# Batches 0 and 1 of a sparse-attention and feed-forward kernel in finer attention phases, and batch 1 hosted by all of tile 0

## The chip, the cores and the metric

The kernel runs on one core of a Trainium2 chip. The metric is the device time of one execution in microseconds (us), as the median of several runs. Engines are named as in the profile: PE is the matmul engine (PEld its weight loads), DVE the vector engine, ACT the scalar engine, POOL the GpSimd engine, SP the engine whose queue issues the loads. The stores are issued from ACT's queue.

## The reference, cut to what matters

Eight batches of 8 heads, 576 positions, head size 64. Heads 0 to 3 look at the last 32 positions (local), heads 4 to 7 at the earlier positions with the same remainder modulo 32 (strided). The result goes through a multiplicative feed-forward stage.

```python
mask_local = (rel >= 0) & (rel < 32)                       # rel = i - j
mask_strided = (rel >= 0) & (j % 32 == i % 32)
scores = where(mask, q @ k.T / 8, -1e9)
x = softmax(scores) @ v                                    # (8, 8, 576, 64) -> (4608, 512)
a = x @ w1; b = x @ w2                                     # 512 -> 1024
out = ((a * b) @ w3) @ w_out                               # 1024 -> 1024 -> 512
```

## The kernel before, in words

**Attention.** A batch is worked in four pairs of heads (hp 0 and 1 local, 2 and 3 strided). The positions of a pair are cut into blocks: 6 of 96 queries (local) or 8 of 72 queries (strided, positions regrouped by remainder), so that only near-diagonal blocks of the scores are computed. A pair has five phases. T (ph_T, L215) transposes q and k of the pair on PE into the PSUM tile pt, and for the first pair of a batch also the last 64 positions of all heads (the rest, R, L232); copies bring them to qT and kT. S (ph_S, L258) computes the scores of all blocks into sps, with the last blocks of each head in pt. The soft part (ph_soft, L278) is an exponential on ACT in two instructions (L286) and one multiplication with the mask on DVE (L287) into ptm. PV (ph_PV, L291) multiplies ptm with v, which carries a column of ones, and DVE divides by the sum: reciprocal (L312), multiplication into xqs (L313); call these two the norm. T2 (ph_T2, L316) transposes xqs, and a copy (L74 or L327 on ACT, L76 on DVE) puts it into xT, the input of the feed-forward stage. Phase function ph_TS (L418) joins S of a pair with T of the next one.

**Feed-forward.** w3 and w_out do not depend on the data, so the kernel first multiplies them into w34 (the fold: fold_tr L389 transposes a block of w3, fold_mm L398 multiplies). Then the 4608 tokens go in 9 tiles of 512. A tile has 24 units: 8 times a (L348) and b (L357), four matmuls of 512 columns each, with the product on DVE (L359), and 8 halves of the output (L371, ops), four matmuls each. Tile t needs the attention of batches 0 to t.

**Order of the work.** PE's program is written out by hand. The attention phases stand in a list, stream, with GAP marks. host (L450) emits the units of the fold or of a tile and takes the phases up to the next marks after each unit. The fold hosts batch 0. Ten of tile 0's a and b units run alone, the other 14 units host batch 1; tile t hosts batch t+1 for t from 1 to 6. T of the next batch's first pair and its S stand at the end of the batch before, except for batches 0 and 1, which both begin with a T of their own.

**Loads.** SP's queue issues the loads in program order; each goes to one of 9 staging tiles in float32 and is cast to float16 by POOL (L78 t for w3, q and k; L185, L196 for v; w2h) or by ACT (w1h, L74). DMA completion semaphores go round in 8 lanes that loads and stores share, so an issue waits for the transfer 8 back. The order at the start is: w3 and w_out with batch 0 between them, w1 and w2 in four parts with batch 1's first q and k group (heads 0 to 3) and rest before the last part, then v of batch 1's local heads (v16L), the second q and k group (heads 4 to 7), v of its strided heads (v16S), and batch 2.

**PSUM.** Eight banks: psF 3 (units), psA 2 (sps, used again by PV), psT 2 (pt), psM 1 (T2, and the last strided block of PV, pm).

## Time and profile before

| | |
|---|---|
| runs | 292.54, 294.87, 295.78 us; median 294.87 us |
| the profiled execution | 296.77 us, its span 295.1 us, mean granted PE clock 0.975 |
| busy, share of the span | PE 90%, DVE 50%, ACT 51%, POOL 35% |
| the fold with batch 0 | to about 48 us |
| tile 0 with batch 1 | about 48 to 84 us |
| tiles 1 to 6 with batches 2 to 7 | about 84 to 250 us |
| tiles 7 and 8 alone | to the end |

The profile's page is one execution. Its view by slices shows busy shares over time, the windows view gives busy time and granted clock for chosen stretches, the timeline lists instructions with the idle time in front of them and what released them (in brackets), the waits view sums such idle time. In a timeline row the first number is the start, the second the time from the start of the first to the end of the last of the instructions that are taken together. The ends of matmuls are modelled, so the distance from one start to the next is the better duration for PE.

### The profile page before, as it was taken

To read this page: it belongs to the slowest core of one execution; us is meant where nothing else is said; L and a number is where in the kernel's file an instruction comes from. 1 tells how busy PE (TensorE), PEld (TensorE's weight loads), DVE (VectorE), ACT (ScalarE), POOL (GpSimd) and SP (SyncE) were. 2 spreads that over 40 slices of the span, in tenths; PEclk is the share of its full clock that TensorE was granted. 3 is DMA by queue.
4 is the path that set the end of the run, shared out by engine and by line. 5 is a ranking of instruction groups with operands and counts; after the bars stand their busy time and mean duration, and the time that the engine had idled before them with its cause. 6 is when DMAs were issued, how large, how long until landed. Compare 5 with 4: busy or idle time off the path is not lost.

```text
span 295.1 us, 6686 instructions
## 1 busy us (share of the span) xinstructions
PE 264.6 (90%) x2689; PEld 135.8 (46%) x2689; DVE 148.4 (50%) x279; ACT 150.2 (51%) x309; POOL 104.6 (35%) x118
## 2 busy tenths in 40 slices
PE   2468987997779999999999999999999999999995
PEld 1133543444445554555455455545554554444442
DVE  2016563474556774765558567646654663330420
ACT  2025784467545556556565655555555655323332
POOL 5649644565445833557566424110000000000000
PEclk9988997999959999999999999999999999999999
DMA  7999999996879957997989892120011002103003
GB/s 247 346 219 344 302 347 264 216 265 122 270 233 224 253 106 206 264 180 243 259 172 286 177 273 49 36 109 3 0 73 74 0 2 107 38 0 138 4 3 142
DMA packets 58656, 48.68 MB, mean 165 GB/s; under 512 B 29184, under 2 KB 49664, under 8 KB 58624
## 3 DMA queue, kind: packets, MB, share of 16 engines
q1 hardware_dynamic: 53440, 38.81, 53.9%
q10 hardware_dynamic: 5184, 9.44, 8.9%
q8 instruction: 21, 0.34, 0.5%
q14 instruction: 11, 0.09, 0.1%
HBM read 38.80 MB, written 9.44 MB: 163 GB/s over the span
## 4 chain that ended last, share of the span: by engine, by line
PE 71%; ACT 10%; DMA 8%; DVE 5%; issue 3%; POOL 1%; SPq 1%
PE bps L357 21%; PE aps L348 20%; PE ops L371 17%; ACT pte L286 4%; PE sps L308 4%; DMA st<-in_moe_w_dram 3%; DMA st<-in_moe_w_out_dram 3%; PE sps L266 2%; DVE ptm L287 2%; PE ps L320 2%; ACT osb L382 2%; PE pt L224 2%; DVE xqs L313 1%; DMA out_dram<-osb 1%; PE pt L266 1%
## 5 line engine op out<-in xcount | busy, mean ns | idle before, releaser
L348 PE MATMUL aps<-xT,w1h 128*128 128x512 f16 x288 | 77.0, 386 | 3.6 <-ACT xT L327 3.6
L351 ACT COPY asb<-aps 128x512 f32<-128x512 f32 x72 | 43.0, 597 | 67.0 <-PE aps L348 65.3
L357 PE MATMUL bps<-xT,w2h 128*128 128x512 f16 x288 | 75.7, 386 | 0.0
L359 DVE TENSOR_TENSOR abt<-bps,asb 128x512 f16<-128x512 f32 x72 | 49.6, 689 | 50.1 <-PE bps L357 48.0
L371 PE MATMUL ops<-w,abt 128*128 128x512 f16 x288 | 68.5, 379 | 0.0
L78 POOL CAST t<-st 128x1024 f16<-128x1024 f32 (+1 forms) x48 | 48.2, 1011 | 32.7 <-DMA st<-in_k_dram 14.5
L357 PEld LDWEIGHTS <-w2h 128*128 128x128 f16 x288 | 26.9, 99 | 35.0 <-issue 7.7
L286 ACT ACTIVATE pte<-sps 128x960 f16<-128x960 f32 (+1 forms) x32 | 31.7, 990 | 19.1 <-PE sps L266 18.0
L348 PEld LDWEIGHTS <-w1h 128*128 128x128 f16 x288 | 26.7, 100 | 28.7 <-issue 1.9
L371 PEld LDWEIGHTS <-abt 128*128 128x128 f16 x288 | 25.9, 98 | 27.7
L185 POOL CAST v16L<-st 32x768 f16<-32x768 f32 (+1 forms) x32 | 27.9, 872 | 22.0 <-PE aps L348 7.6
L382 ACT COPY osb<-ops 128x512 f32<-128x512 f32 x36 | 21.5, 598 | 25.8 <-PE ops L371 25.8
L313 DVE TENSOR_TENSOR xqs<-sps,rcp 96x768 f16<-96x768 f32 (+1 forms) x32 | 32.6, 1018 | 0.7
L287 DVE TENSOR_TENSOR ptm<-pte,maskL 128x1152 f16<-128x1152 f16 x16 | 13.6, 852 | 28.7 <-ACT pte L286 28.7
L287 DVE TENSOR_TENSOR ptm<-pte,maskS 72x1152 f16<-72x1152 f16 x16 | 14.8, 928 | 25.6 <-ACT pte L286 25.6
L74 ACT COPY qT<-pt 128x256 f16<-128x256 f16 (+2 forms) x64 | 23.3, 410 | 7.7 <-PE pt L232 4.5
L196 POOL CAST v16S<-st 72x1024 f16<-72x1024 f32 x16 | 17.8, 1116 | 21.5 <-PE pm L308 11.6
L308 PEld LDWEIGHTS <-ptm 72*128 72x128 f16 (+1 forms) x448 | 18.2, 98 | 14.7 <-DVE ptm L287 7.1
L371 PE MATMUL ops<-woh,w3T 128*128 128x512 f16 x64 | 19.6, 438 | 2.1 <-POOL woh L78 1.2
L266 PEld LDWEIGHTS <-kT 64*128 64x128 f16 x448 | 10.1, 97 | 16.2 <-issue 10.6
L320 PEld LDWEIGHTS <-xqs 72*128 72x128 f16 (+1 forms) x224 | 12.0, 99 | 8.1 <-DVE xqs L313 1.6
L76 DVE COPY kT<-pt 128x128 f16<-128x128 f16 (+1 forms) x28 | 11.5, 435 | 7.5 <-ACT qT L74 7.5
(53 smaller groups left out, 201.1 us busy)
## 6 DMA issues: line engine op xcount, KB each, us to landing
out_dram<-osb ACTq DMA_DIRECT2D x36, 256.0 KB, 2.0
st<-in_moe_w_dram SPq DMA_DIRECT2D x16, 512.0 KB, 8.7
st<-in_q_dram SPq DMA_DIRECT2D x16, 512.0 KB, 5.3
st<-in_k_dram SPq DMA_DIRECT2D x16, 512.0 KB, 6.3
st<-in_v_dram SPq DMA_DIRECT2D x32, 144.0 KB, 7.1
st<-in_v_dram SPq DMA_DIRECT2D x16, 256.0 KB, 7.4
st<-in_moe_w_out_dram SPq DMA_DIRECT2D x4, 512.0 KB, 8.1
st<-in_q_dram SPq DMA_DIRECT2D x8, 128.0 KB, 7.8
```

Of the source, the lines that this page charges most:

```text
L78: nc.gpsimd.tensor_copy(out=out, in_=in_)
L185: nc.gpsimd.tensor_copy(out=vt[pr, hs, :, 0:D], in_=st[pr])
L286: nc.scalar.activation(out=pte[0:kr, lo:hi], in_=src, func=AF.Exp, bias=0.0, scale=scale)
L287: nc.vector.tensor_mul(ptm[0:kr, 0:2 * S].rearrange("p (a x) -> p a x", x=w), pte[0:kr].rearrange("p (a x) -> p a x", x=w), _ap(mk, 0, [[m ...
L308: pe(nc.tensor.matmul(xps[:, h, i * 65:i * 65 + 65], s.ptm[0:kr, c0:c0 + P], vt[0:kr, 2 * (s.hp % 2) + h, c, :], start=True, stop=True))
L313: nc.vector.tensor_mul(s.xqs[0:w, cs[0]:cs[0] + l].rearrange("p i h d -> p h i d"), xv[:, :, :, 0:D], _ap(rcp, 0, [[rcp.ap[0][0], w], [ST, ...
L348: pe(nc.tensor.matmul(aps, w1h[:, ci, bass.ds(jc * P, P)], xT[ci][:, tok], start=(ci == 0), stop=(ci == KM - 1)))
L351: nc.scalar.copy(out=asb, in_=aps)
L357: pe(nc.tensor.matmul(bps, w2h[:, ci, bass.ds(jc * P, P)], xT[ci][:, tok], start=(ci == 0), stop=(ci == KM - 1)))
L359: nc.vector.tensor_mul(abts[tch][:, jc, :], bps, st["asb"])
L371: pe(nc.tensor.matmul(st["ps"], lhs(ci), rhs(ci), start=(ci == 0), stop=(ci == KF - 1)))
L382: nc.scalar.copy(out=osb, in_=ps)
```

## The change

For batches 0 and 1 only, the phases are new. ah_T transposes q and k of a pair in 128-row transposes (8 instead of 16) into psM, and ACT copies both out; ah_R does the same for the rest (4 instead of 8). ah_S computes the scores in two groups g of half the blocks, each in a PSUM tile of its own with one exponential and one masked multiplication of half the size. ah_PV, one call for each group, has its own PSUM tile and its own norm. psA and psT become one pool, psB, with two tiles that all of these (and sps and pt of the later batches) use in turn; psM now also carries the transposes of batches 0 and 1. ptm gets 64 columns more, zeroed once.

The list for batches 0 and 1 has no marks: spread emits units and takes items at an even rate. Tile 0 hosts batch 1 with all its units: 3 a and 3 b units, then 18 units among the phases. Batch 2 begins with a T of its own (ph_TS with no S). For the later batches T2 of the pair before stands after one mark behind S and T instead of two, and one mark more stands behind it; PV keeps its place.

In the built program the order of the loads on SP and of the casts on POOL is the same as before. On PE the order at the end of tiles 2 to 6 is also the same as before (S, T, a unit, T2, first a of the next tile), since no unit falls on the last mark; inside a tile T2 comes one unit sooner. At the end of tile 1 all units stand before S, T and T2. In batch 1 PE's order is: a b a b a b, T(0), a, R, b, T(1), a, S(0), b, PV(0) group 0, a, PV(0) group 1, b, T(2), a, S(1), b, T2(0), a, PV(1) group 0, b, PV(1) group 1, o, T(3), o, S(2), o, T2(1), o, PV(2) both, o, S(3), o, T2(2), o, PV(3) both, o, T2(3), where the number is the pair and o a half of the output.

```diff
-    psA = ctx.enter_context(tc.tile_pool(name="psA", bufs=1, space=bass.MemoryType.PSUM))
-    psT = ctx.enter_context(tc.tile_pool(name="psT", bufs=1, space=bass.MemoryType.PSUM))
+    psB = ctx.enter_context(tc.tile_pool(name="psB", bufs=2, space=bass.MemoryType.PSUM))
...
+    def ah_T(s):
+        ps = psM.tile([P, 2, NM], FP16, tag="m")
+        for i, nm in enumerate("qk"):
+            src = x16[(s.b, nm, s.hp // 2)]
+            h0 = 2 * (s.hp % 2)
+            for c in range(4):
+                pe(nc.tensor.transpose(ps[:, i, c * P:(c + 1) * P],
+                                       src[:, c, h0:h0 + 2].rearrange("p h d -> p (h d)"), id16))
+        for i, t in enumerate((qT, kT)):
+            if s.local:
+                c0 = 32 * i
+                nc.scalar.copy(out=t[:, s.hp, c0:c0 + NM].rearrange("x (p c) -> x p c", c=4),
+                               in_=ps[:, i].rearrange("x (c p) -> x p c", c=4))
+            else:
+                nc.scalar.copy(out=t[:, s.hp, 0:S].rearrange("x (u c w) -> x u c w", u=2, c=4)[:, :, :, 0:64],
+                               in_=ps[:, i].rearrange("x (c t u) -> x u c t", c=4, u=2))
...
+    def ah_S(s):
+        w, kr = s.w, s.kr
+        m = s.n // 2
+        for g in range(2):
+            sps = psB.tile([P, 2, NB], FP32, tag="big", name="sps")
+            for i in range(m):
+                ks = w * (g * m + i)
+                for h in range(2):
+                    r = half_rows(h)
+                    pe(nc.tensor.matmul(sps[:, h, i * w:(i + 1) * w], kT[r, s.hp, ks:ks + P],
+                                        qT[r, s.hp, ks:ks + w], start=True, stop=True))
+            pte = att.tile([P, 2, 288], FP16, tag="pte", bufs=2)
+            mk = maskL if s.local else maskS
+            nc.scalar.activation(out=pte[0:kr], in_=sps[0:kr, :, 0:288], func=AF.Exp, bias=0.0, scale=scale)
+            nc.vector.tensor_mul(ah_ptm(s, g)[0:kr, 0:S].rearrange("p (a x) -> p a x", x=w),
+                                 pte[0:kr].rearrange("p h (a x) -> p (h a) x", x=w),
+                                 _ap(mk, 0, [[mk.ap[0][0], kr], [0, s.n], [1, w]]))
+
+    def ah_PV(s, g):
...
+        xps = psB.tile([P, 2, NB], FP32, tag="big", name="xps")
+        for i in range(m):
+            for h in range(2):
+                c0 = h * 288 + i * w
+                pe(nc.tensor.matmul(xps[:, h, i * 65:(i + 1) * 65], ptm[0:kr, c0:c0 + P],
+                                    vt[0:kr, 2 * (s.hp % 2) + h, g * m + i, :], start=True, stop=True))
...
+        norm(s, xps[0:w, :, 0:m * 65], g * m, m)
...
+        if b < AHEAD:
+            if i == 0:
+                add(ah_T, s)
+                add(ah_R, b)
+                add(ah_T, pairs[p + 1])
+            add(ah_S, s)
+            if i:
+                add(ph_T2, pairs[p - 1])
+            add(ah_PV, s, 0)
+            add(ah_PV, s, 1)
+            if i < 2:
+                add(ah_T, pairs[p + 2])
+            if i == 3:
+                add(ph_T2, s)
+                batch_end[b] = len(stream)
+            continue
+        if i == 0 and b == AHEAD:
             add(ph_TS, None, s)
             gaps(2)
...
         add(ph_TS, s, t)
-        gaps(2)
-        if i or b >= AHEAD:
+        gaps(1)
+        if i or b > AHEAD:
             add(ph_T2, pairs[p - 1])
             if i == 0:
+                gaps(1)
                 batch_end[b - 1] = len(stream)
-        gaps(1)
+        gaps(1 if i == 0 and b > AHEAD else 2)
         add(ph_PV, s)
...
+    def spread(units, upto, lead=0):
+        n = len(units) - lead
+        p0 = pos[0]
+        for i, u in enumerate(units):
+            u()
+            tgt = p0 + ((upto - p0) * max(i + 1 - lead, 0)) // n
+            while pos[0] < tgt:
+                stream[pos[0]]()
+                pos[0] += 1
...
-    host(fold, batch_end[0], lead=3)
+    spread(fold, batch_end[0], lead=3)
     load_qk(2, 0)
     load_rest(2)
     load_vL(2)
-    host(ab_halves(0), pos[0] + 11, lead=9)
+    units = ab_halves(0) + o_halves(0)
+    p0, n = pos[0], batch_end[1] - 1 - pos[0]
+    spread(units[0:16], p0 + n * 11 // 19, lead=4)
     load_qk(2, 1)
     load_vS(2)
-    host(o_halves(0), batch_end[1])
+    spread(units[16:23], p0 + n)
+    units[23]()
+    stream[pos[0]]()
+    pos[0] += 1
```

More of the change, by code (lines that the diff above doesn't have):

```diff
@@ L418, in ph_TS @@
     def ph_TS(s, t):
-        pt = psT.tile([P, 2, NB], FP32, tag="t")
-        after = []
         if s is not None:
-            after.append(ph_S(s, pt))
+            pt, soft = ph_S(s)
+            after = [soft]
+        else:
+            pt = psB.tile([P, 2, NB], FP32, tag="big", name="pt")
+            after = []
         if t is not None:
```

59 lines of the change are left out of this document (40 added, 19 removed).

## The prediction

> **What bounds the kernel now.** I read the page first, then the windows view by stage, then what PE waited for.
>
> ```profile
> span 295.1 us, 6686 instructions
> PE 264.6 (90%) x2689; PEld 135.8 (46%) x2689; DVE 148.4 (50%) x279; ACT 150.2 (51%) x309; POOL 104.6 (35%) x118
> PE 71%; ACT 10%; DMA 8%; DVE 5%; issue 3%; POOL 1%; SPq 1%
> ```
> ```profile
> 26.33:48.01 21.68, 17.89 (x244) 10.44 (x245) 13.73 (x25) 14.62 (x29) 12.09 (x12) 1.00 1.09 315
> 48.01:84.31 36.30, 31.10 (x366) 16.09 (x362) 18.43 (x33) 20.84 (x43) 20.21 (x22) 0.92 0.90 218
> 115.05:142.59 27.54, 26.71 (x309) 14.15 (x308) 17.81 (x34) 15.73 (x34) 17.66 (x18) 1.00 0.97 229
> ```
>
> PE is the bound (90% busy, 71% of the chain of waits). The windows rows are: stretch, its length, busy us of PE, PEld, DVE, ACT and POOL, the granted PE clock, DMA share, GB/s. A later tile (third row) takes 27.54 us for 24 units and one batch of attention and PE idles 0.83 in it. Tile 0 with batch 1 (second row) takes 36.30 for the same kind of work and a little of batch 2. So 5 us idle and a clock of 0.92 stand in one stage; the fold's stage before it has 3.8 idle. What PE waited for, before and after 48 us:
>
> ```profile
> PE sps L308 <- DVE ptm L287: 2.6, 2, 1.5
> PE ps L320 <- DVE xqs L313: 0.7, 1, 0.7
> ```
> ```profile
> PE sps L308 <- DVE ptm L287: 2.7, 3, 1.2
> PE pt L266 <- DVE kT L76: 1.7, 1, 1.7
> ```
>
> These are latencies: PV waits for exponential and mask, S for a transposed k. They also cost clock. In the next rows the clock (third figure from the end) is halved twice, and each time the 3.4 us just before held little PE work:
>
> ```profile
> 42.20:45.60 3.40, 1.91 (x20) 0.90 (x19) 1.44 (x2) 3.40 (x6) 1.04 (x1) 1.00 1.10 349
> 44.40:47.80 3.40, 1.62 (x23) 0.89 (x24) 2.30 (x5) 2.27 (x5) 1.04 (x1) 1.00 1.20 268
> 47.80:51.40 3.60, 3.60 (x17) 1.42 (x18) 0.00 (x0) 1.23 (x2) 2.08 (x2) 0.53 1.12 253
> 78.60:82.00 3.40, 1.52 (x20) 0.79 (x20) 3.09 (x6) 2.18 (x6) 1.88 (x3) 1.00 0.50 169
> 82.00:88.60 6.60, 5.78 (x57) 3.27 (x58) 3.15 (x8) 2.80 (x5) 2.34 (x3) 0.51 0.90 263
> ```
>
> Busy 1.62 of 3.40 (48%) and 1.52 (45%) preceded a fall, 1.91 (56%) did not. The half clock cost about 1.7 us of work after 48 and 3 us after 82.
>
> **The change, part by part.** PE durations are distances between starts:
>
> ```profile
> 33.52 0.61 PE L393 MATMUL trp<-id,t 128*128 128x128 f16 x8
> 33.97 1.03 PE L371 MATMUL ops<-woh,w3T 128*128 128x512 f16 x4
> 118.96 0.21 PE L266 MATMUL pt<-qT,kT 64*128 64x96 f16 x1
> 119.22 0.40 PE L224 MATMUL pt<-id,t 64*128 64x64 f16 x16
> 119.55 1.04 PE L357 MATMUL bps<-xT,w2h 128*128 128x512 f16 x4
> 120.42 1.03 PE L348 MATMUL aps<-xT,w1h 128*128 128x512 f16 x4
> 121.29 0.42 PE L320 MATMUL ps<-id,xqs 96*128 96x96 f16 x6
> 121.54 1.03 PE L357 MATMUL bps<-xT,w2h 128*128 128x512 f16 x4
> 122.41 0.53 PE L308 MATMUL sps<-v16L,ptm 128*128 128x65 f16 x12
> 122.78 1.02 PE L348 MATMUL aps<-xT,w1h 128*128 128x512 f16 x4
> ```
>
> A unit is 0.87, S 0.26, T 0.33, T2 0.25, PV 0.37 (12 matmuls; 16, so strided, an estimate of 0.49). Eight 128-row transposes take 0.45, as the fold's show, against 0.33 for the sixteen that they replace: the new T is dearer by 0.12 on PE, about 1 us over eight pairs. The Trainium skill ("TensorE: Matmul & The Clock Gate", Part 3: Packing small matmuls) says that weight loads overlap running matmuls only in another row group, which speaks against the 128-row form; by that rule, the trace agrees with 0.45 against 0.33.
>
> *Latency.* S to PV now: two exponentials and one mask.
>
> ```profile
> 29.90 0.97 ACT L286 ACTIVATE pte<-sps 128x960 f16<-128x960 f32 x1 [0.99 <-PE sps L266]
> 30.77 0.33 ACT L286 ACTIVATE pte<-pt 128x192 f16<-128x192 f32 x1
> 31.13 0.76 DVE L287 TENSOR_TENSOR ptm<-pte,maskL 128x1152 f16<-128x1152 f16 x1 [1.11 <-ACT pte L286]
> 33.72 0.23 DVE L312 RECIPROCAL rcp<-sps 96x12 f32<-96x12 f32 x1 [1.50 <-PE sps L308]
> 33.98 0.95 DVE L313 TENSOR_TENSOR xqs<-sps,rcp 96x768 f16<-96x768 f32 x1
> ```
>
> That is 2.0 us (29.90 to 31.89). From these rows a group of 576 needs about 0.65 on ACT and 0.4 on DVE, so group 0 is ready after 1.1 and group 1 after 1.7. PE has two units and T2 (1.99) between S and PV in batch 1, and as much or a block of the fold in batch 0: those waits (2.6 and 2.7) go. The instructions on DVE and ACT double in number, but ACT is at 20.84 of 36.30 and DVE at 18.43, so their added fixed time lies beside PE.
>
> *Batch 0.* Of the 21.68 us, 2.6 goes, two T cost 0.24 more, and the last T2 still waits for its norm (about 1.0, 0.7 before, now with no unit in front of it). Tile 0 begins at about 46 to 47 instead of 48.01; both ends matter little, because of what comes next.
>
> *Batch 1: the load that is late next.* SP's and POOL's orders are unchanged, and no copy or store is put ahead of these loads. Before, they landed so:
>
> ```profile
> 55.04 0.48 SPq L163 DMA_DIRECT2D st<-in_k_dram  x1
> 56.40 3.44 POOL L185 CAST v16L<-st 32x768 f16<-32x768 f32 x4 [0.15 <-POOL w2h L78]
> 59.91 1.03 POOL L78 CAST t<-st 128x1024 f16<-128x1024 f32 x1
> 61.75 1.09 POOL L78 CAST t<-st 128x1024 f16<-128x1024 f32 x1 [0.81 <-DMA st<-in_k_dram]
> ```
>
> DMA share is above 1 from 26 to 51 (rows above), so I take these times as fixed. The second k group is cast by 62.84. In the new order T(2), which needs it, stands behind 12 units, T(0), R, T(1), S(0) and PV(0): 12 x 0.87 + 2 x 0.45 + 0.25 + 0.26 + 0.37 = 12.2, and about 2 of hand-overs (R waits for the copies of T(0), T(1) for those of R, all in the one bank of psM; PV(0) for v16L, about 58.5, or for its mask, about 59). From 46.5 that is 60.7 to 61.2. T(2) then waits about 1.7 for k and starts at 62.85, and everything queued on PE behind it waits too. So a gain in batch 0 up to that size is lost here.
>
> Behind T(2)'s start stand 12 units (10.44), T(2) and T(3) (0.90), three S (0.78), four T2 (1.00), PV (0.37 + 0.49 + 0.49 = 1.35); the parts listed leave 0.13 a pair unexplained in the third windows row (26.71 - 24 x 0.87 - 5.3, by four), so 0.45 more: 14.92. Waits: S(3) group 1 needs the bank that PV(2) group 1's norm frees (two norms of about 0.85, an estimate: two thirds of 0.95 and a reciprocal of 0.2, behind 0.87 of unit: 0.5); the last T2 waits for two norms with one unit over them (0.7); the first a waits for the copy of xT (0.25, below). Sum 62.85 + 14.92 + 1.45 = 79.2; the first a of tile 1 ends at 80.1.
>
> *Tile 1 and the end of tiles.*
>
> ```profile
> 86.16 1.91 PE L357 MATMUL bps<-xT,w2h 128*128 128x512 f16 x4
> 108.87 0.22 PE L308 MATMUL pm<-v16S,ptm 72*128 72x65 f16 x2 [0.16 <-ACT xT L327]
> 113.34 0.81 PE L348 MATMUL aps<-xT,w1h 128*128 128x512 f16 x3
> 114.10 0.68 ACT L327 COPY xT<-ps 128x576 f16<-128x576 f16 x1
> 114.83 0.38 PE L348 MATMUL aps<-xT,w1h 128*128 128x512 f16 x1 [0.68 <-ACT xT L327]
> ```
>
> Before, the first a of tile 1 ended at 86.16: a lead of 6.05. Tile 1 then has to do what before stood ahead of it: two T, R, S of batch 2 (1.25), and S waits about 0.35 (an estimate; the same wait took 1.7 before, waits rows above) for copies of k that stand on DVE behind a product. It does not run at half clock: 1.2 back (86.16 to 88.60 at 0.5). At its end all units precede S, T and T2, so fewer lie over the exponential that ACT does before xT: 0.4 lost (0.87 less cover, one copy of 0.48 less in ACT's queue). At the other tile ends PE's order is the same and the wait of 0.68 is ACT's, whose order there is the same too: T2's half unit brings nothing there, against 3.4 if those five waits went. Inside tiles the 0.16 before pm goes: 0.5 in all.
>
> **Sum.** 6.05 - 1.25 - 0.35 + 1.2 - 0.4 + 0.5 = 5.75. The profiled execution took 296.77 (span 295.1 and 1.67 around it); 291.0 is its counterpart, and scaled by 294.87/296.77 to the median of the runs, 289.1.
>
> The unknown is the clock while T(2) waits. The worst 3.4 us there hold two units and half of PV(0), about 1.76 by distances between starts, about 1.95 as the page counts ends: nearest to the row with 1.91, that did not fall. So I take no fall (0); the other end is one half-clock stretch of 3.4 to 6.6 us, 1.7 to 3.3. The Trainium skill ("TensorE: Matmul & The Clock Gate", Part 1: The HAM clock gate) lets the clock halve after an idle window of about 3.4 us; by that rule no wait left here is long enough and the sum stays. This trace is stricter: it fell with 45 and 48% busy, so the measurement decides and the fall stays a rival.
>
> **The rivals.**
> (a) *The clock falls at T(2)'s wait.* For it: 48% was enough at 47.8. Against: 56% was not. Gain 5.75 less 1.7 to 3.3: 290.8 to 292.4.
> (b) *The loads do not hold T(2).* If the second k group lands earlier, up to the 1.7 us of waiting go: 287.4. Against: nothing in the load order moves.
> (c) *It only shifts the waits.* If POOL's and DMA's times slip, each us is a us at T(2); 3 us later and the gain is under 1%: 292 to 295. For it: DMA ran saturated. Against: same order, same bytes, no store ahead of them.
> (d) *Slower: psM hands over late.* One bank now carries T, R and T2 of batches 0 and 1, and only ACT empties it. About 12 hand-overs fall where PE has nothing else; with ACT's queue (exponentials, w3 and w1 casts) each would have to come 0.5 later than I count to eat the gain and 0.75 to make it slower by over 1%: 298. Against: ACT is 67% and 57% busy in the two stages (14.62 of 21.68, 20.84 of 36.30).
>
> **Numbers.** Forecast 0.50, (a) 0.25, (b) 0.08, (c) 0.11, (d) 0.06. About 1% is what a measurement of this kernel can tell from no change. Faster by over 1% (under 291.9): forecast, (b) and nearly all of (a), 0.82; within 1%: (c) and the rest of (a), 0.13; slower 0.05. The range goes from 286.6, which takes in (b) and a spread of about 1 between runs, to 291.9, which takes in most of (a).
>
> **What would show it.** The a and b units of tile 0 start near 47 at full clock; no wait of PV on ptm above 0.5; T(2) of batch 1 released by POOL at about 62.8 after 1 to 2 us of idle PE; first a of tile 1 near 79; clock 1.00 from 48 on; waits of 0.68 unchanged at the ends of tiles 2 to 6. I am wrong if T(2) is not held by a load, if PE waits on ACT's copies out of psM by over 3 us together, or if the clock is at 0.5 for more than one stretch behind 48 us.

## The result, and the profile after

The changed kernel takes 292.64 us in the median of 20 runs (289.84 to 297.26) against 294.81 (292.05 to 299.72) for the kernel before on the same chip: a ratio of 0.9913, 95% interval 0.9883 to 0.9942. It is faster, by about 0.9%. (Ratios, here and below, leave out the runs more than 1.5% above the fastest of the same kernel; medians and ranges are of all runs.) The forecast was 289.1 us, 1.9%, and the range ended at 291.9. The profiled execution of the changed kernel took 292.48 us, span 290.8; that of the kernel before 296.77, span 295.1. So the profiled pair differs by 4.29 us, where the sum of the prediction had 5.75, and the medians by 2.2.

The head of the page after, and its windows by stage (batch 0 with the fold, tile 0 with batch 1, tile 2), columns as before:

```profile
span 290.8 us, 6556 instructions
PE 264.0 (91%) x2617; PEld 136.8 (47%) x2617; DVE 150.0 (52%) x293; ACT 151.3 (52%) x305; POOL 103.4 (36%) x118
```
```profile
24.60:46.03 21.43, 19.24 (x244) 11.47 (x242) 15.48 (x33) 15.68 (x27) 12.38 (x12) 0.99 1.07 328
46.03:79.97 33.94, 30.18 (x277) 15.46 (x275) 17.87 (x36) 19.48 (x38) 19.26 (x21) 0.95 1.04 222
111.33:138.56 27.23, 26.56 (x310) 14.08 (x308) 18.20 (x35) 15.88 (x34) 17.87 (x19) 1.00 0.98 237
55.80:59.20 3.40, 1.70 (x19) 0.74 (x19) 1.76 (x4) 2.12 (x5) 3.12 (x5) 1.00 0.98 272
59.20:62.60 3.40, 2.59 (x15) 1.26 (x15) 1.64 (x4) 0.46 (x1) 1.99 (x3) 0.52 1.06 234
```

Tile 0 starts at 46.03 instead of 48.01 and hands over at 79.97. Tile 2 takes 27.23 instead of 27.54. The last two rows show one stretch at half clock, behind one in which PE was busy for 1.70 of 3.40 us. What PE waited for between 46 and 86:

```profile
PE xps L374 <- DVE v16L L187: 1.6, 1, 1.6
PE ps L392 <- DVE xqs L385: 1.3, 2, 0.8
PE xps L374 <- DVE ptm L361: 0.9, 1, 0.9
PE pt L268 <- DVE kT L76: 0.5, 1, 0.5
PE ps L336 <- ACT kT L325: 0.3, 1, 0.3
```

The waits before (2.7 for ptm, 1.7 for kT) have gone down to 0.9 and 0.5. The first row is new. PE and POOL where the prediction put the load (PE first, then the casts):

```profile
58.15 0.24 PE L374 MATMUL xps<-v16L,ptm 128*128 128x65 f16 x2 [0.88 <-DVE ptm L361]
60.01 0.38 PE L374 MATMUL xps<-v16L,ptm 128*128 128x65 f16 x4 [1.63 <-DVE v16L L187]
60.20 1.90 PE L420 MATMUL aps<-xT,w1h 128*128 128x512 f16 x4
61.89 0.54 PE L374 MATMUL xps<-v16L,ptm 128*128 128x65 f16 x6
62.24 1.27 PE L429 MATMUL bps<-xT,w2h 128*128 128x512 f16 x4
63.34 0.61 PE L320 MATMUL ps<-id,t 128*128 128x128 f16 x8
...
79.97 1.27 PE L420 MATMUL aps<-xT,w1h 128*128 128x512 f16 x4
```
```profile
59.84 1.04 POOL L78 CAST t<-st 128x1024 f16<-128x1024 f32 x1
62.23 1.04 POOL L78 CAST t<-st 128x1024 f16<-128x1024 f32 x1 [1.35 <-DMA st<-in_k_dram]
```

The second k group is cast by 63.27, T(2) of batch 1 starts at 63.34, 0.07 later, and the first a of tile 1 16.63 us behind it. T(2) shows no idle time of its own: the half clock and the wait for v16L had already used it up.

For the comparisons below, the first b of tiles 0, 1 and 2, and how long tiles 0, 1 and 2 take from first b to first b (in the changed order, the first b of tile 1 stands behind T and R of batch 2 too), with the end of the cast of that k group and what remains from it to the end of the span (in the kernel before, no wait of PE is for that cast, so there the last figure also holds how early tile 0 started against it):

| profile | first b of tile 0 | tile 0 | tile 1 | tile 2 | cast of k ends | cast to end | clock, 46 to 90 |
|---|---|---|---|---|---|---|---|
| before | 49.70 | 36.46 | 28.89 | 27.54 | 62.84 | 232.3 | falls at 48 and 82 |
| before, second (b_again) | 48.58 | 36.17 | 28.85 | 27.60 | 62.76 | 230.9 | 0.68 in 80 to 90 |
| before, third (b_third) | 49.93 | 35.03 | 27.37 | 27.55 | 63.77 | 228.7 | 1.00 |
| before, fourth (b_p4) | 47.76 | 35.74 | 29.12 | 27.84 | 63.24 | 230.0 | 0.83 in 80 to 90 |
| before, fifth (b_p5) | 47.97 | 36.28 | 30.78 | 27.80 | 63.62 | 231.7 | 0.66 in 80 to 90 |
| after | 47.14 | 34.49 | 29.70 | 27.23 | 63.27 | 227.5 | fall at 59 |
| after, second (a_again) | 46.46 | 34.54 | 29.92 | 27.23 | 62.97 | 227.3 | 1.00 |
| after, third (a_p3) | 49.80 | 33.02 | 30.34 | 27.24 | 64.34 | 228.3 | 1.00 |

### The profile page after: what moved, and what is told of

It is laid out like the page before. It is cut to its first block, busy times and chain, and to the rows that moved or that the text cites. A ratio compares the mean times of both kernels' runs of the same rounds, so it can differ in the third digit from the quotient of the medians.

```text
span 290.8 us, 6556 instructions
## 1 busy us (share of the span) xinstructions
PE 264.0 (91%) x2617; PEld 136.8 (47%) x2617; DVE 150.0 (52%) x293; ACT 151.3 (52%) x305; POOL 103.4 (36%) x118
## 4 chain that ended last, share of the span: by engine, by line
PE 73%; ACT 10%; DMA 6%; DVE 6%; issue 3%; SPq 1%; POOL 0%; ACTq 0%
PE ops L443 22%; PE bps L429 20%; PE aps L420 19%; DMA st<-in_moe_w_dram 3%; PE sps L310 3%; DMA st<-in_moe_w_out_dram 3%; PE ps L392 2%; PE sps L268 2%; ACT xT L399 2%; ACT pte L360 2%; DVE xqs L385 1%; PE pt L225 1%; ACT pte L288 1%; ACT osb L454 1%; PE pt L268 1%
## 5 line engine op out<-in xcount | busy, mean ns | idle before, releaser
L423 ACT COPY asb<-aps 128x512 f32<-128x512 f32 x72 | 42.5, 590 | 63.8 <-PE aps L420 61.5
L429 PE MATMUL bps<-xT,w2h 128*128 128x512 f16 x288 | 74.3, 380 | 0.0
L454 ACT COPY osb<-ops 128x512 f32<-128x512 f32 x36 | 21.3, 592 | 29.9 <-PE ops L443 27.3
L186 POOL CAST v16L<-st 32x768 f16<-32x768 f32 (+1 forms) x32 | 27.5, 861 | 16.5 <-DMA st<-in_v_dram 8.5
L288 ACT ACTIVATE pte<-sps 128x960 f16<-128x960 f32 (+1 forms) x24 | 23.8, 990 | 11.8 <-PE sps L268 10.8
L385 DVE TENSOR_TENSOR xqs<-sps,rcp 96x768 f16<-96x768 f32 (+1 forms) x24 | 24.5, 1020 | 0.5
L197 POOL CAST v16S<-st 72x1024 f16<-72x1024 f32 x16 | 16.9, 1059 | 18.2 <-PE pm L310 13.8
L289 DVE TENSOR_TENSOR ptm<-pte,maskL 128x1152 f16<-128x1152 f16 x12 | 10.0, 832 | 21.8 <-ACT pte L288 21.8
L289 DVE TENSOR_TENSOR ptm<-pte,maskS 72x1152 f16<-72x1152 f16 x12 | 10.2, 854 | 19.5 <-ACT pte L288 19.5
L74 ACT COPY qT<-pt 128x256 f16<-128x256 f16 (+2 forms) x48 | 17.5, 409 | 0.9 <-DVE kT L76 0.9
L310 PEld LDWEIGHTS <-ptm 72*128 72x128 f16 (+1 forms) x336 | 13.6, 97 | 6.3 <-issue 0.6
L392 PE MATMUL ps<-id,xqs 72*128 72x72 f16 (+1 forms) x224 | 13.9, 201 | 1.3 <-DVE xqs L385 1.3
L76 DVE COPY kT<-pt 128x512 f16<-128x512 f16 (+1 forms) x24 | 10.7, 467 | 4.8 <-ACT qT L74 4.8
```

Source lines behind the costliest of these rows:

```text
L186: nc.gpsimd.tensor_copy(out=vt[pr, hs, :, 0:D], in_=st[pr])
L288: nc.scalar.activation(out=pte[0:kr, lo:hi], in_=src, func=AF.Exp, bias=0.0, scale=scale)
L310: pe(nc.tensor.matmul(xps[:, h, i * 65:i * 65 + 65], s.ptm[0:kr, c0:c0 + P], vt[0:kr, 2 * (s.hp % 2) + h, c, :], start=True, stop=True))
L385: nc.vector.tensor_mul(s.xqs[0:w, c0:c0 + l].rearrange("p i h d -> p h i d"), xv[:, :, :, 0:D], _ap(rcp, 0, [[rcp.ap[0][0], w], [ST, 2], [ ...
L392: pe(nc.tensor.transpose(ps[:, t * w:(t + 1) * w], s.xqs[0:w, t].rearrange("p h d -> p (h d)"), id16[0:w, 0:w]))
L423: nc.scalar.copy(out=asb, in_=aps)
```

## The experiments

The theory after the result: T(2) is held by the load as predicted, and what is missing is that the kernel before, as profiled, had lost time to its clock that it does not always lose. Rivals: the load is a side matter and the latencies count; the hosting by all of tile 0 counts; something in tile 1 takes the gain back. Ratios are to the kernel before on the same chip.

**The kernel before against itself, b_again.** No edit.

> The kernel before, unchanged, profiled a second time. Theory A (the profiled execution of before was not a typical one: it was 2 us above the median, and the excess is the 6.6 us of half clock after 82): the first b of tile 1 at 84 to 85 instead of 86.16, half clock there for at most one stretch of 3.4 us, span about 293. Theory B (that execution was typical, and the shortfall of the gain lies in the changed kernel): the half clock of 6 us or more after 82 comes again and the span is near 295. Ratio 1.000 within 0.003 by both.

Ratio 0.9962 (0.9928 to 0.9997), 294.71 us: what differs by 0.4% can't be told from no change here. Its profile has half clock for 6.8 us again, from 79.7 (0.68 over 80 to 90), as theory B said, but a span of 293.7, nearer to theory A.

**The change again, a_again.** No edit.

> The changed kernel, unchanged, profiled a second time. Both theories: ratio about 0.991. If the load of v holds PV(0) and the load of k holds T(2) (theory load): T(2) of batch 1 starts within 0.2 us after POOL's cast of the second k group, at 62.8 to 63.5, whether or not the clock falls before it, and the first a of tile 1 starts 16.5 us later. If the fall of the clock sets it (theory clock): T(2) starts 1 us or more later than the cast in the executions with a fall.

Ratio 0.9889 (0.9839 to 0.9939), 292.47 us. Here the clock stayed at 1.00, and the second half of T(2) was released by POOL at 63.03 after 1.0 us of idle PE, 0.06 behind the cast. The end came 227.3 us behind the cast, against 227.5 with the fall: the fall at 59 cost nothing.

**The load earlier, v_early.**

```diff
-    load_w12(3)
     load_vL(1)
+    load_w12(3)
```

> The changed kernel with the v load of batch 1's local heads issued ahead of the last part of w1 and w2. It lands some 3 us earlier, so PV(0) does not wait for it (1.63 us before). Theory load (k holds T(2), the rest has slack): T(2) keeps its time, 62.8 to 63.5, the wait moves to T(2) with POOL as its releaser, 2 to 3 us, and the time is that of the changed kernel within 0.5 us, ratio 0.989 to 0.993. Theory clock/v (the wait for v and the half clock behind it cost the end): 1.6 to 3 us faster than the changed kernel, ratio 0.981 to 0.986.

Ratio 0.9868 (0.9799 to 0.9937), but from three of its six runs: the six took 290.75 to 296.25 us, median 294.21, and the profiled one, span 289.0, is the fastest of them. In its profile the wait for v16L is gone and POOL releases T(2) (PE, then POOL):

```profile
61.78 0.40 PE L320 MATMUL ps<-id,t 128*128 128x128 f16 x4 [0.91 <-POOL t L78]
```
```profile
60.68 1.04 POOL L78 CAST t<-st 128x1024 f16<-128x1024 f32 x1 [1.62 <-DMA st<-in_k_dram]
```

The edit moved more than v: the cast of k came 1.55 us earlier than in the profile after, so T(2) did not keep its time, as the theory had expected. The span is 1.8 shorter, so in this execution the end goes with the cast (227.3 behind it). The runs do not show a gain over the change: the ratio's interval takes in that of the change, and the median of all six is above the change's.

**More units ahead of T(2), lead6 and lead10.** Lead is the number of units of tile 0 ahead of T(0). lead10 has ten, so that few units are left among the phases.

```diff
-    spread(units[0:16], p0 + n * 11 // 19, lead=4)
+    spread(units[0:16], p0 + n * 11 // 19, lead=6)
```

> The changed kernel with two more units of tile 0 ahead of the first phase of batch 1 (lead 6 instead of 4; T(2) stands behind 13 units instead of 12). Theory load: T(2) still starts at 62.8 to 63.5 but with one unit less behind it, so 0.9 us faster than the changed kernel, ratio about 0.988. Theory latency (hand-overs and exponentials in batch 1 set the pace): no gain or a loss, since fewer units stand between the phases, ratio 0.991 to 0.996.

> The changed kernel with ten units of tile 0 ahead of batch 1's phases, as before the change (the hosting by all of tile 0 undone, the finer phases kept). Theory load: T(2) stands behind 14 units instead of 12, so it does not wait for k; two units (1.7 us) less are left behind it, but S and PV of the first two pairs stand with nothing between, which costs 1 to 2 us. Tile 0 within 1 us of the changed kernel's 34.5 us, ratio 0.988 to 0.994. Rival (spreading all 24 units is what saves the time in tile 0): tile 0 takes 2 us longer, ratio 0.996 to 1.000.

lead6: 0.9945 (0.9896 to 0.9993); lead10: 1.0001 (0.9963 to 1.004). Filling T(2)'s wait with units gained nothing, and ten units ahead lost the whole gain. Neither profile shows PE waiting on POOL any more; lead10 waits 1.5 for an exponential, 2.7 for norms (1.4 and 1.3) and 0.9 for the copy of kT instead. Its profiled execution is the fastest of its twelve, and tile 0 takes 34.69 us in it, about as in the profile after, so the profile does not show where the loss of the others lies. The load theory's gain for lead6 did not come. lead6's profiled execution is one of the slower half of its runs, so its longer waits for norms (2.0, 1.3 in the profile after) and its half clock from 61.5 to 65 explain nothing by themselves. That units moved ahead of T(2) are missing between the later phases is argued, not tried.

**One part alone, fine0 and host1.** fine0 has the new phases for batch 0 only, batch 1 as before. host1 is fine0 with the old phases of batch 1 hosted by nearly all of tile 0.

```diff
-        if b < AHEAD:
+        if b < 1:
...
-    units = ab_halves(0) + o_halves(0)
-    p0, n = pos[0], batch_end[1] - 1 - pos[0]
-    spread(units[0:16], p0 + n * 11 // 19, lead=4)
+    ab = ab_halves(0)
+    for u in ab[0:10]:
+        u()
...
+    host(ab[10:16], mid)
...
+    host(o_halves(0), batch_end[1])
```

> The new phases for batch 0 alone; batch 1 in the phases and the hosting of before (ten units of tile 0 alone, then 14 among its phases), with T2 of the changed kernel. Theory load (in the changed kernel the lead won in batch 0 is lost again where T(2) of batch 1 waits for k): here T(2) comes later than k in any case, so the lead of batch 0 (2 us at the first b of tile 0) is kept to the end, tile 0 takes 36 us from its first b to that of tile 1 as before, and the gain is 2 to 2.8 us, ratio 0.990 to 0.994, nearly that of the whole change. Rival (the gain comes from batch 1's phases and hosting): under 1 us, ratio 0.997 to 1.000.

> Batch 0 in the new phases; batch 1 in the phases of before, but hosted by 20 of tile 0's units (four run ahead instead of ten). Theory load: T(2) now stands behind 9 to 10 units and waits 3 to 4 us for the second k group (released by POOL at about 63), so hosting alone gains nothing over fine0: ratio 0.993 to 0.998. Rival (hosting by all of tile 0 hides the latencies of the old phases and gains by itself): tile 0 shorter by 1 us or more than fine0's 36.1, ratio under 0.991.

fine0: 0.9926 (0.9883 to 0.9969); host1: 0.9921 (0.9887 to 0.9954). Batch 0 alone brings nearly all that the change measures (0.9913 and 0.9889), and hosting by more of tile 0 adds nothing that can be told. So the new order of batch 1 adds nothing measurable in time to that of batch 0. It fits that in the old order batch 1 can keep batch 0's lead, and that the new one waits for it at T(2); in fine0's profile PE waits nowhere on POOL between 44 and 86. host1's waits for POOL are 1.1 us at T(2) and 0.4 elsewhere, not the 3 to 4 that were expected.

The profiles also show what batch 0 gains. In the five of the kernel before (table above) the first b of tile 0 comes at 48.8 us in the mean, 10.8 behind the last cast of w3; in the twelve of kernels with the new batch 0 it comes at 47.6, 9.7 behind that cast. So the lead is a little over 1 us, with 0.8 to 1.0 of spread (standard deviation) between executions.

**The ends of the tiles, t2_end and t2_old.** In t2_end, T2 stands directly behind S and T at the end of a tile and a unit stands behind it; t2_old puts the T2 of the later batches back where it was.

```diff
-        gaps(1)
+        if i or b == AHEAD:
+            gaps(1)
...
-                gaps(1)
+                gaps(2)
...
-            mid = marks[len(marks) // 2 - 1] + 1
+            mid = marks[len(marks) - 13] + 1
```

> The changed kernel with T2 of a batch's last pair directly behind S and T of the next batch, and a unit of the old tile behind T2, for tiles 1 to 6. Theory (the waits of 0.68 at the ends of tiles, 1.2 at the end of tile 1, stay in the changed kernel because no unit fell between T2 and the next tile): the waits of the first a for xT fall from 4.1 us together to under 1, tiles 2 to 6 take 26.6 to 26.8 us from first b to first b instead of 27.23, 3 to 3.5 us faster than the changed kernel, ratio 0.977 to 0.982. Rival (ACT's queue sets xT whatever PE does): waits of 0.5 or more stay, under 1 us faster.

> The changed kernel with T2 of batches 2 to 7 in its old place (two marks behind S and T). One look. Theory: the waits of PV's last block (pm) for the copy of xT come back, tiles 2 and 3 take 27.3 to 27.5 us from first b to first b instead of 27.23, and the waits of 0.68 at the ends of tiles 2 to 6 are as in the changed kernel. Rival: no difference, 27.23.

t2_end: 0.987 (0.9816 to 0.9924), 291.85 us. Tiles 3 and 5 take 26.75 and 26.74 instead of 27.23 and 27.24, but tile 2 takes 27.90 instead of 27.23 (the last section shows what came between). The waits for xT fall from 4.1 to 1.2 together, and from the cast of k to the end it is 225.9 instead of 227.5: half of the 3 to 3.5 that were expected. t2_old: one run, 295.47 us; its tile 2 takes 28.21, more than the 27.3 to 27.5 that were expected, its tiles 3 to 5 take 27.33, 27.76 and 27.33 as in the kernel before, and the waits for xT stay at 4.1. So the unit by which the change moves T2 gives 0.1 a tile and does not touch the wait at the end.

**T(2) behind PV(1), k_late, and both gains together, v_t2.** k_late is v_early with T(2) and T(3) of batch 1 behind PV(1); v_t2 is v_early with the edit of t2_end.

```diff
-            if i < 2:
+            if i < 2 and b == 0:
                 add(ah_T, pairs[p + 2])
+            if i == 1 and b == 1:
+                add(ah_T, pairs[p + 1])
+                add(ah_T, pairs[p + 2])
```

> The changed kernel with v of batch 1 loaded ahead of the last part of w1 and w2, and T(2) and T(3) of batch 1 put behind PV(1), so that nothing on PE needs the second k group before about 65. Theory load (the landing of k sets tile 0's end): no wait for POOL is left in tile 0, 1 us faster than v_early's tile 0 (32.8 us from first b to first b), 31.5 to 32; ratio 0.980 to 0.986. Rival (the hand-overs and exponentials set the pace): tile 0 stays at 32.8 or more, with waits on ptm in place of the wait for k.

> The two changes that gained, together: v of batch 1 ahead of the last part of w1 and w2, and T2 directly behind S and T at the ends of tiles 1 to 6 with a unit behind it. If they add: the span ends 227.4 us after the cast of batch 1's second k group as in the changed kernel's executions, less 1.7 for the ends of tiles; span 287.5 to 289, ratio 0.978 to 0.985. If v's place does nothing, the same as t2_end (ratio 0.987).

k_late: 0.9872 (0.9829 to 0.9914), no better than v_early although no wait for POOL is left: tile 0 takes 33.15, where the load theory expected 31.5 to 32, with 1.8 us of waits for ptm, as the rival said, and tile 1 31.81. So in that order the landing of k does not set the end of tile 0. (Its profiled execution, 294.29 us, is slower than its median, 292.84.) v_t2: 0.9859 (0.9814 to 0.9903), 291.15 us, span 288.0. Its ratio is the lowest of these kernels, and from the cast of k to the end it is 226.0, 1.4 less than the changed kernel's 227.4, about what t2_end gave. The intervals do not separate it from v_early, t2_end or the change, from which it differs by 0.3 to 0.5%.

**Is the clock the missing part? b_third, b_p4, b_p5, a_p3.** The kernel before three times more, the change once more; no edits.

> The kernel before, a third profile. Theory (the execution that the prediction was made against had its early loads, up to the last cast of w3, 1 us later than usual; the stages behind are the same in every execution): the last cast of w3 ends at 37 to 37.5 instead of 38.01, the span is 293 to 294.2, and it ends 256.5 to 257 us after that cast. Rival (the excess is spread over the later stages): the distance from that cast to the end differs by 1 us or more from 257.1.

> Edit: none, the kernel before, a fourth profile. Theory (its half clock is a matter of where the thin stretches fall, which shifts from run to run): either a clock below 1.00 in 48 to 51 and 82 to 88 and about 65.2 us from first b of tile 0 to first b of tile 2, or 1.00 throughout and about 62.4; nothing in between but one fall of two, about 63.5 to 64. Rival: the same stage length of 65.2 whatever the clock.

> Edit: none, the kernel before, a fifth profile, with what was said for the fourth. With five profiles the theory expects at least two with falls and at least one without, and the time profiled to follow: about 2.5 to 3 us shorter, counted from the last cast of w3, where there is no fall.

> Edit: none, the kernel after, a third profile. Theory: T(2) of batch 1 starts with the end of the cast of the second k group, and the span is 227.4 us more than that (227.5 and 227.3 in the first two), whether or not the clock falls ahead of it; first b of tile 1 comes 81.6 less 63.3 = 18.3 us behind the cast. Rival: the span follows the start of tile 0 (244 us behind its first b), and not the cast.

Windows of the third profile of the kernel before, at the same two places where the first one fell, and its tile 0:

```profile
45.00:48.40 3.40, 1.52 (x20) 0.79 (x20) 2.21 (x5) 2.47 (x5) 1.04 (x1) 1.00 1.19 278
48.40:51.80 3.40, 3.16 (x21) 1.54 (x22) 0.79 (x2) 1.27 (x3) 1.78 (x2) 1.00 1.17 229
78.00:81.40 3.40, 1.52 (x20) 0.79 (x20) 3.07 (x6) 2.19 (x6) 2.30 (x2) 1.00 0.93 268
48.83:82.88 34.05, 29.00 (x366) 15.07 (x363) 18.04 (x33) 20.44 (x43) 20.26 (x22) 1.00 0.97 226
```

PE was busy for 1.52 of 3.40 us, as little as ahead of the falls in the first profile, and the clock did not fall. The same 366 matmuls of tile 0 take 29.00 us instead of 31.10. Tiles 0 and 1 together take 62.40 here and 65.35, 65.02, 64.86 and 67.06 in the four profiles with a fall. The expected size of one fall (63.5 to 64 for the two tiles) was too small: b_p4 and b_p5 had one each and lost 2.5 and 4.7. Not all of this is the clock. In the two tiles PE is busy for 55.71 us in b_third, 59.31 in the first profile, 57.54 in b_p4 and 58.65 in b_p5: the half clock added 3.6 in the first and 1.8 and 2.9 in the others, and the rest of their loss, 0.6 and 1.7, is idle time of PE (the last section has a cause for such time). The time from the k cast to the end is 228.7 without a fall and 230.0 to 232.3 with. Nor was it the early loads, as the theory for b_third had it: the last cast of w3 ended later in b_third (38.86) than in the first two profiles (38.01 and 37.19), and yet the end came 253.6 us behind it instead of 257.1 and 256.5. The change ends 253.3 behind that cast.

The Trainium skill ("TensorE: Matmul & The Clock Gate", Part 1: The HAM clock gate) says that the window over which activity is judged is free-running and does not restart with the kernel. The traces agree and show more. In each of the eighteen traces of this document, all changes of the clock lie whole multiples of 3.413 us apart; in the first profile of the kernel before it falls at 47.94 and 82.08, ten windows apart. Between these edges, the thin stretch at the end of batch 1 reads so in the first and in the third profile (the first row is of the first):

```profile
78.67:82.08 3.41, 1.52 (x20) 0.79 (x20) 3.17 (x6) 2.11 (x6) 1.89 (x3) 1.00 0.48 161
```
```profile
76.94:80.35 3.41, 2.23 (x25) 0.98 (x22) 2.06 (x5) 2.62 (x6) 1.31 (x1) 1.00 1.10 337
80.35:83.77 3.42, 1.86 (x40) 1.11 (x40) 2.26 (x7) 1.88 (x4) 2.08 (x2) 1.00 0.38 134
```

In the first the stretch filled one window, in the third an edge cut it in two, and no window was thin enough. Over the eighteen traces, from 26 us to 8 us before the end, the ten falls came behind windows with PE busy for 0.94 to 1.80 us, and of the others at full clock only four had less than 1.80 (1.60 to 1.77). So whether the same thin stretch halves the clock depends on where it lies between the edges, and that shifts from run to run. The same part of that page of the Trainium skill also says that the clock halves after at least one idle window; here it halved behind windows in which PE was busy for up to 53%, and the measurement decides.

a_p3 ends 228.3 behind the cast where 227.4 was expected. Its rival (244 us behind the first b of tile 0) is off by 1.2, so the end alone decides little. At the first b of tile 1, though, 82.82, the theory (18.3 behind the cast, 82.64) is off by 0.2, and tile 0 is 1.5 shorter than in the first profile. The excess comes in tile 1 (30.34 instead of 29.70): a masked product took 1.55 us where the profile after has 0.75, and PE waited 0.81 for the copy of xT queued behind it on DVE, 0.17 in the profile after. Batch 0 ran late here (first b of tile 0 at 49.80, clock 0.66 from 20 to 30), so T(2) came when k was there:

```profile
63.32 1.03 PE L429 MATMUL bps<-xT,w2h 128*128 128x512 f16 x4
64.18 0.61 PE L320 MATMUL ps<-id,t 128*128 128x128 f16 x8
...
98.29 1.55 DVE L289 TENSOR_TENSOR ptm<-pte,maskS 72x1152 f16<-72x1152 f16 x1 [1.17 <-ACT pte L288]
101.34 0.22 PE L310 MATMUL pm<-v16S,ptm 72*128 72x65 f16 x2 [0.81 <-DVE xT L76]
```

T(2) starts without a wait and tile 0 takes 33.02 instead of 34.49. So 1.5 us of batch 0's lead are lost at T(2) where tile 0 starts at 46 to 47, as the prediction said.

**The clock kept up in the kernel before, b_warm.** Matmuls that nobody reads, where PE waited at the ends of batches 0 and 1.

```diff
+    def ph_warm(n):
+        wps = psF.tile([P, NT], FP32, tag="f", name="wps")
+        for i in range(n):
+            pe(nc.tensor.matmul(wps, id16, w34[:, 0, :], start=True, stop=True))
...
+        if i == 0 and b == AHEAD:
+            add(ph_warm, 7)
         add(ph_TS, s, t)
...
+        if i == 3 and b < AHEAD:
+            add(ph_warm, 6 - b)
         add(ph_PV, s)
...
+            if b == 0:
+                add(ph_warm, 3)
             add(ph_T2, s)
```

> Edit: the kernel before, with matmuls that nobody reads put on PE where it waits at the ends of batches 0 and 1: six ahead of PV of pair 3 of batch 0, three ahead of its last T2, five ahead of PV of pair 3 of batch 1, seven ahead of the first S of batch 2 (each 128x512, 0.22 us; the waits there were 1.49, 0.73, 1.17 and 1.71). Nothing else moves, and no work of the kernel is left out. Theory (what the change gained in tile 0 is mostly the half clock that follows these thin stretches in the kernel before, and it comes in some executions and not in others): the granted clock is 1.00 from 48 to 115 in the profile, the three stretches of 3.4 us that held 1.5 to 1.6 us of PE now hold over 2.5, first b of tile 0 to first b of tile 2 is about 62.4 us as in the third profile of the kernel before (65.35 and 65.02 in the two with falls), span about 292.5, ratio 0.991 to 0.994 against the kernel before, with a narrower spread of its times. Rival (the gain is the order's own, latencies and hosting; the clock is a side matter): the ratio is 0.997 to 1.003, since the dummies only fill waits.

Ratio 1.0012 (0.9972 to 1.0053), 294.61 us: the theory's ratio missed. Its clock part held. The windows over the two thin stretches and the stage:

```profile
44.72:48.12 3.40, 2.40 (x26) 1.19 (x25) 1.85 (x4) 2.38 (x4) 1.04 (x1) 1.00 1.09 346
78.50:81.90 3.40, 2.79 (x34) 1.47 (x33) 1.88 (x2) 2.20 (x4) 1.65 (x2) 1.00 1.00 298
48.00:115.00 67.00, 61.14 (x698) 31.47 (x696) 40.12 (x70) 38.04 (x81) 38.47 (x40) 1.00 0.98 216
```

The clock is 1.00 throughout (though the first stretch held 2.40 where over 2.5 was expected), and over its 12 runs the mean granted clock is 0.994, where that of the kernel before beside it is 0.984. But the dummies do not only fill waits: the two tiles took 65.01 us (50.81 to 115.82) instead of 62.4, with PE busy for 58.70 and idle for 6.31, where b_third has 55.71 and 6.69. Twelve of them stand behind 48 us, 12 x 0.22 = 2.6 us of PE, and some waits are still there behind them:

```profile
81.36 0.59 PE L308 MATMUL sps<-v16S,ptm 72*128 72x65 f16 x14 [0.61 <-DVE ptm L287]
...
85.02 0.39 PE L266 MATMUL sps<-qT,kT 64*128 64x96 f16 x10 [0.49 <-DVE xqs L313]
...
87.72 0.38 PE L348 MATMUL aps<-xT,w1h 128*128 128x512 f16 x1 [1.02 <-ACT xT L327]
```

The profiled execution, at 297.45 us, is the slowest of the twelve, so its span says little of the price. What a fall costs is therefore not settled by this kernel.

**All executions together.** Each execution has a mean granted clock beside its time. In the four groups of experiments the kernel before ran 101 times: 293.9 us in the median of the 20 executions with a clock of 0.99 or more, 297.3 in that of the 27 below 0.978. A straight line through all 199 executions of these groups (one constant for each group, one for each kernel, one slope) gives 1.9 us for 0.01 of clock, standard error 0.16. By it:

| kernel | executions | mean clock | against before, us | the same at equal clock, us |
|---|---|---|---|---|
| before | 101 | 0.983 | 0 | 0 |
| change | 7 | 0.991 | -3.0 (0.7) | -1.3 (0.55) |
| fine0 | 12 | 0.988 | -2.1 (0.6) | -1.4 (0.45) |
| host1 | 12 | 0.984 | -2.1 (0.6) | -2.0 (0.5) |
| lead6 | 12 | 0.990 | -0.7 (0.6) | +0.8 (0.45) |
| lead10 | 12 | 0.990 | -0.1 (0.6) | +1.0 (0.45) |
| v_early | 6 | 0.991 | -2.0 (0.8) | -0.3 (0.6) |
| k_late | 12 | 0.994 | -3.1 (0.6) | -1.3 (0.5) |
| t2_end | 6 | 0.992 | -3.9 (0.8) | -2.5 (0.6) |
| v_t2 | 6 | 0.989 | -4.4 (0.8) | -3.5 (0.6) |
| b_warm | 12 | 0.994 | -0.8 (0.6) | +1.0 (0.5) |

(Standard errors in brackets.) By this fit the change gains a little over 1 us by its order and somewhat more by its clock; b_warm gains about as much by its clock and gives 1.0 back for its dummies. Without the 38 executions more than 1.5% above the fastest of their kernel it gives 1.4 us for 0.01 of clock, and for the change 2.4, of which 1.4 (0.46) by its order. The 20 runs of the change in the first comparison are not in it; ten of those have the clock 0.994 and take 290.53 to 295.50 us, so the clock is not all that spreads the times. A fit is no experiment: the split between order and clock is good to about 1 us, and stays open beyond that.

## Why the prediction was wrong

Step by step, in the prediction's own order.

- *Batch 0, tile 0 begins at 46 to 47.* Right: 46.03. Part of it is the execution: over all profiles the new batch 0 brings a little over 1 us, where 48.01 to 46.03 is 2. The waits for ptm went from 2.6 to 0.7 in batch 0; that no wait of PV on ptm would be above 0.5 was wrong (0.7 and 0.9).
- *T(2) waits for k, then starts at 62.85.* Right: at the end of the cast in the profile after (63.34 behind 63.27), released by POOL in a_again, v_early, t2_end and v_t2 after 0.9 to 1.9 us. The cast itself was 0.43 later than before.
- *PV(0) for v16L, about 58.5.* Wrong: 60.01. The copy of v16L stands on DVE behind two masks and a product (rows in the last section), and PE waited 1.6. In this execution it was hidden, because T(2) had to wait for k anyway; in v_early it is gone.
- *No fall of the clock.* Wrong in the profile after, right in a_again and a_p3: rival (a) happened at 59.3, and cost nothing where the prediction priced it at 1.7 to 3.3, because it lay inside the wait for k.
- *T(2) to the first a of tile 1: 14.92 of work and 1.45 of waits, 16.37.* Nearly right: 16.63 to the start of that a, and 0.24 waited inside it for xT (its four matmuls take 1.27 instead of 1.03), 16.87.
- *Tile 1: 1.25 and 0.35, and 0.4 at its end.* Under-sized, by 0.9 where the clock does not enter. The third profile of the kernel before has no half clock to disturb the comparison. In it the first a of tile 1 ends at 84.96, 21.2 us behind the k cast; in the profile after at 81.08 (79.97, 0.87 and 0.24), 17.8 behind it: 3.4 gained by then, 2.3 of it by the earlier start of tile 0 against the cast. From there to the first b of tile 2 the change takes 30.25 (81.08 to 111.33) instead of 27.37, so tile 1 gives 2.9 back where 2.0 were counted. Its PE rows, with the places of the added work:

```profile
81.17 0.41 PE L225 MATMUL pt<-id,t 64*128 64x64 f16 x16
81.41 0.28 PE L233 MATMUL pt<-id,t 64*128 64x64 f16 x8
81.63 1.04 PE L429 MATMUL bps<-xT,w2h 128*128 128x512 f16 x4
82.50 1.03 PE L420 MATMUL aps<-xT,w1h 128*128 128x512 f16 x4
83.98 0.21 PE L268 MATMUL pt<-qT,kT 64*128 64x96 f16 x1 [0.46 <-DVE kT L76]
84.27 0.39 PE L268 MATMUL sps<-qT,kT 64*128 64x96 f16 x10
84.48 0.20 PE L268 MATMUL pt<-qT,kT 64*128 64x96 f16 x1
84.50 0.42 PE L225 MATMUL pt<-id,t 64*128 64x64 f16 x16
84.85 1.04 PE L429 MATMUL bps<-xT,w2h 128*128 128x512 f16 x4
...
111.11 0.38 PE L420 MATMUL aps<-xT,w1h 128*128 128x512 f16 x1 [1.18 <-ACT xT L399]
```

T and R take 0.55 (81.08 to 81.63), S with the second T 1.48 (83.37 to 84.85) with 0.46 of waiting where 0.35 was estimated; S alone takes 0.52 here instead of 0.26. The wait at the end is 1.18 where the third profile has 0.67 (0.5 more, 0.4 predicted).

- *Tiles 2 to 6, 0.5 together, and waits of 0.68 that stay.* Right: 27.23 against 27.54 for tile 2, then 0.1 a tile, and 4.1 us of waits for xT in six pieces in the whole profile.
- *"A lead of 6.05" and "1.2 back" for the half clock.* Against the profiled execution the lead was 5.08 (86.16 less 81.08), 1.0 short, by the later start of T(2) and by what came behind it. What failed is that this execution, in which the clock fell twice, stood for the kernel before. The third profile, without a fall, takes 35.03 from the first b of tile 0 to that of tile 1 instead of 36.46, and 27.37 for tile 1 instead of 28.89: 1.4 of the 6.05 were the falls, and tile 1 had another 1.5, of which the prediction took 1.2. So 2.6 of the 5.75 were credited to taking away something that the kernel before does not always pay. Against the third profile 3.4 by the end of that a, less 2.9 in tile 1, and 0.7 behind it (from the first b of tile 2 to the end 179.5 instead of 180.2) make 1.2: what the two profiles show from the cast to the end (228.7 less 227.5), and near the 1.3 of the fit.
- *"Scaled by 294.87/296.77 to the median."* This is the step that carried that error into the forecast, by 1.9 us. The profiled execution of the kernel before was 1.9 above its median, with a clock of 0.975 where the mean is 0.983. The forecast had already taken its falls away, so 291.0 should not have been scaled down with the median of the kernel before as well. The change's own profiled execution, 292.48, stands at its median, 292.64.

So the sum missed in the profiled pair by 1.46 (5.75 less 4.29): 0.5 by the later start of T(2), 0.5 from there to the end of the first a, 0.5 by tile 1 (111.33, a lead of 3.72 over 115.05, where the terms made 5.25, 6.05 - 1.25 - 0.35 + 1.2 - 0.4), 0.1 back in the later tiles. The larger part of the miss in the median, 1.9 of 3.5, is the base against which it was set: an execution with two falls, which was then treated as a typical one. Rivals (b) and (d) did not happen; (c), the loads slipping, happened by 0.43.

## What to carry to other kernels

Before a gain is counted from one profile, ask which of the lost time is in every execution: a stretch at half clock behind a thin stretch may be absent in the next run of the same program, and the mean clock of each run, set against its time, tells how much of the spread it makes. Where a load holds the path (here, in the changed kernel, the cast of the second k group), compare executions from that load; where none does, compare the length of a stage, split into busy and idle time of the engine that bounds it. Do not scale a profiled time by the median of a kernel whose lost time the change has already been credited with. Work taken out of a stage with waits and put into a full one is paid there at full price and with its hand-overs, so price the stage that receives it from its own rows.

## What the runs showed of the hardware that was not expected

The clock can stay at 1.00 behind a stretch of 3.4 us with PE busy for 45% of it, and fall behind an equal one in another execution, because its changes keep to edges 3.413 us apart (the rows of the experiments on the clock). The kernel before ran at mean clocks from 0.966 to 0.994 on one program, and from 292.3 to 301.8 us.

A copy of 0.84 us on DVE held PE for 1.6 us. It stood behind three other instructions in DVE's queue, and a cast ran on POOL beside it. DVE's rows in the profile after, and POOL's:

```profile
57.41 0.69 DVE L361 TENSOR_TENSOR ptm<-pte,maskL 128x576 f16<-128x576 f16 x1 [2.14 <-ACT pte L360]
58.02 0.68 DVE L431 TENSOR_TENSOR abt<-bps,asb 128x512 f16<-128x512 f32 x1
58.62 0.47 DVE L361 TENSOR_TENSOR ptm<-pte,maskL 128x576 f16<-128x576 f16 x1
59.12 0.84 DVE L187 COPY v16L<-v16L 32x640 f16<-32x640 f16 x1
```
```profile
56.09 3.69 POOL L186 CAST v16L<-st 32x768 f16<-32x768 f32 x4
```

Splitting the mask in two for a shorter latency put one more instruction ahead of that copy.

Two instructions of DVE, the masked product and this copy, take longer when POOL is at work as they start. In the eighteen traces, from 24 us on, the product of 1152 columns takes 0.75 to 0.76 us in all 328 cases in which POOL was idle at its start, and over 1.15, up to 1.62, in 82 of the 157 in which it was not; the copy takes 0.32 to 0.33 against up to 1.20. DVE's multiplication of the norm, which reads PSUM, shows nothing of the kind (96x768: 0.95 to 0.96 us in all 244). This is a second source of spread beside the clock: between 46 and 142 us the first and third profiles of the kernel before have none of the long products, b_p4 and b_p5 five and four, and the slow tile 2 of t2_end holds one, that of t2_old two. No experiment moved a cast away from a product, so what it would save is not shown.

The same kernel measured against itself gave 0.9962 (0.9928 to 0.9997), an interval that does not hold 1: differences of half a per cent need more than one such comparison.
